# Two elementwise products of chunk 1 moved from VectorE to GpSimd in an attention and two-layer MLP kernel

## The chip, the cores and the metric

The kernel runs on one core of a Trainium2 chip. The metric is the device time of one execution in microseconds (us). The engines are named as in the profile: PE is TensorE (PEld its weight loads), DVE is VectorE, ACT is ScalarE, POOL is GpSimd, and SP is SyncE, which here issues nearly all DMAs. Each engine works through its own queue in order and waits at the head of it for what the instruction needs.

## The reference

A gated linear attention over 768 steps is followed by two MLP layers. Per batch entry and head (4 x 8, width 48), cut to what matters:

```python
mag = np.sqrt(a_re * a_re + a_im * a_im)
scale = np.minimum(mag, 0.999) / (mag + 1e-06)
a_re_n, a_im_n = (a_re * scale, a_im * scale)
for t in range(S):
    new_re = ar * S_re - ai * S_im
    new_im = ar * S_im + ai * S_re
    S_re, S_im = (new_re + kv, new_im)          # kv = outer(k_t, v_t)
    y[:, :, t] = np.einsum('bhd,bhde->bhe', q[:, :, t], S_re)
# the result, as x (3072 x 384), goes through two layers:
h = x @ w_in; x = (h - np.tanh(h)) @ w_out      # layer 0, width 2048
h = x @ w_in; r = np.maximum(h, 0.0); x = (r * r) @ w_out   # layer 1
```

## The kernel before, in words

**Attention.** The 768 steps are cut into 6 chunks of 128. A *unit* is one chunk of one batch entry, so there are 24: unit n has c, b = divmod(n, 4). Chunk 0 is units 0 to 3, chunk 1 is units 4 to 7. In a unit the gate is taken to polar form. Step `a0` loads `ri` (real and imaginary part side by side, 128 x 768). `a1` squares it into `ab`, and `a2` makes on ACT, out of `ab`, one over the real part (tile half `A`). `a3` multiplies the imaginary part by it (`im` times `A`, 128 x 384, in place in `ri`) and bounds the logarithm of the magnitude (`ab<-ab,ri`). `a4` takes the arctangent on ACT (`ri<-ri`), `a5c` adds the phase carried from the chunk before (`ri<-cr,ri`, one partition), `a6l` and `a6` sum along the chunk on PE (`pc` and `pu`), and `a7x` makes the exponentials of the summed logarithm, `ee`. Step `a8x` multiplies the loaded `qk` (q and k, 128 x 768) by `ee` in place. `a9` multiplies by cosine and sine (`kn<-qk,fg`, `qn<-qk,fg`), `a10` transposes on PE (`pk`, `pq`) and ACT copies out (`kqT`), `a11` makes scores (`sc`), which DVE masks (`wm<-sc,maskab`), and `a12` and `a13` make the output `px` and the state's update `pU`.

**MLP.** A block is one of 16 slices m of the hidden width, for one of 6 groups of 512 tokens, in one of 2 layers. Nine products into `h` are followed by tanh on ACT (`t<-h`), a subtraction on DVE (`t<-h,t`), a split into a rounded part `gh` (ACT) and a rest `gl` (DVE), and nine products into `acc`, two blocks later. The `h` tiles of this stage take turns in two PSUM buffers, so the products of block m+2 begin once DVE's `t<-h,t` has read block m's `h`. In layer 0's first group the weights are made meanwhile: per block DVE does one `cv<-st` and two `cv<-st,cv` (128 x 768), ACT a cast to `wh`, and DVE `wl<-cv,wh`.

**What sets the order.** Chunk 1's units are spread over the 16 steps beside layer 0's first group (`plan`, `attn`, `block_step`, tables `AHEAD` and `JOINS`). In this stretch the wrapper `Turn`, which elsewhere forces DVE's and PE's order to be that of the code, is off for all but the last block, so the framework's scheduler orders each engine's queue by its own estimates. Helper `Turn.issue` records all operations on `dve`, `ten`, `sp` and `act_e` under line 155. Tiles tagged `qk` and `ee` have one buffer each outside chunk 0's early units; those tagged `ri` have three. GpSimd clears tiles at the start and splits layer 1's inputs (`xh<-xf`, line 351) six times. In between its queue is empty.

Of the kernel before, what the change touches and what calls it, by code (L numbers as in the profile page):

```python
# [17 lines left out]
ALU = mybir.AluOpType  # L18
# [25 lines left out]
def kernel(  # L44
# [9 lines left out]
    nc = tc.nc  # L54
# [106 lines left out]
    ten, dve, sp = (Turn(e) for e in (nc.tensor, nc.vector, nc.sync))  # L161
# [237 lines left out]
    def unit(n):  # L399
        c, b = divmod(n, B)  # L400
# [10 lines left out]
        V = {}  # L411
# [60 lines left out]

        def a3():
            Bt, im = V["B"], V["im"]
            dve.tensor_tensor(im, im, V["A"], op=ALU.mult)
            dve.scalar_tensor_tensor(
                Bt, Bt, 2.0 * LOG_RMAX, V["X"], op0=ALU.min, op1=ALU.subtract
            )
# [106 lines left out]
                f()  # L585

        def a8x():
            dve.tensor_tensor(V["qk"], V["qk"], V["ee"], op=ALU.mult)


        def a9(pairs=(("kn", "k"), ("qn", "q"))):
# [192 lines left out]
        if c == 0:  # L784
            return dict(
                ld=a0, sq=a1, ln=a2, ph=a3, pc=a6l, ee=a7x, at=a4, pu=a6, rd=a7, lq=l2, lv=l3,
                qe=a8x, sn=a8, er=a7r, kn=lambda: a9((("kn", "k"),)), qn=lambda: a9((("qn", "q"),)),
                t0=t0, e0=t0v, t1=t1_, e1=t1v, s0=lambda: a11((0,)), s1=lambda: a11((1,)),
                m0=lambda: a11v((0,)), m1=lambda: a11v((1,)),
                px=a12, x=a12v, pU=a13, st=a13v, ff=fill,  # L790
            )
        if not packed:
            return [
                (i, dict(p=1, e=5.1, v=5.2, p2=6.1, v2=6.2, k=5.05 if b == B - 1 else 5.1)[kind], f) for i, kind, f in (
                    (0, "e", a0), (1, "e", a1), (2, "e", a2), (3, "e", a3), (4, "e", a3b),
                    (5, "p2", a6l), (6, "e", a7x), (6, "e", l2), (7, "e", a4), (7, "e", a5),
                    (8, "p2", a6), (8, "v2", a7), (10, "e", a8x), (10, "e", a7r),
                    (10 if b == B - 1 else 12, "e", a8), (12, "e", l3), (11 if b == B - 1 else 12, "k", a9),
                    (13, "p", t0), (13, "v", t0v), (13, "p2", t1_), (13, "v2", t1v),
                    (14, "p", a11), (14, "v", a11v), (15, "p", a12), (15, "p", a13),  # L800
                    (15, "v", a12v), (15, "v", a13v),
                )
            ]
# [7 lines left out]
        return [  # L811
            (-1, 2.05, a0), (1, 5.2, a1), ln + (a2,),
            ph + (a3,), (5, 5.1, a3b), (6, 6.3 if late < 2 else 1.1, a6l),
            (6, 1.4, a0c), ex + (a7x,), (7, 6.2, l2), at + (a4,), {0: (9, 5.95), 1: (9, 5.02)}.get(late, (at[0], 7.1)) + (a5c,),
            er + (a7r,), (9, 7.2 if first else 5.3, a5s), (9, 6.9 if late == 1 else 5.4, a8x),
            (10, 6.25 if first else 1.1, a6), (10, 6.26 if first else 1.2, a7),
            (11, 5.15 if first else 1.45, lambda: table("silu_and_others")),
# [9 lines left out]
    for n in range(B, NU):  # L827
        c, b = divmod(n, B)
# [423 lines left out]
```

## Time and profile before

| | us |
|---|---|
| median of 3 runs | 981.78 (981.53 to 982.27) |
| the profiled execution, whole | 981.58 |
| its span, first to last instruction | 979.5 |
| PE busy within it | 950.2 |
| DVE busy | 546.2 |
| ACT busy | 631.6 |
| POOL busy | 19.3 |

About 2 us of an execution lie around the span. PE is busy nearly all the time, DVE and ACT about half of it on average, yet not evenly. A busy time is the union of an engine's instructions, so two that overlap by a little count once. A timeline row gives start, duration, engine and operation, and in brackets how long the engine sat idle before it and what ended that.

### The profile page before, as it was taken

The page shows a single profiled execution, that of the slowest core. Times are in us where ns is not written, and L with a number is a line of the kernel's source. Part 1 is how long each engine was busy: PE and PEld are TensorE (multiplying, and loading weights), DVE is VectorE, ACT ScalarE, POOL GpSimd, SP SyncE. Part 2 cuts the span into 40 slices and gives each one's busy share as a digit, 9 for nine tenths or more (in the row PEclk, how much of TensorE's full clock was granted, in tenths as well). Part 3 has the DMA queues.
Part 4 walks back from the last instruction along what each step waited for, and adds up shares of the span by engine and source line. Part 5 has one row for each costly group of instructions (what it writes and reads, how often), then busy time and mean ns, then how long its engine had stood idle before and what let it go on. Part 6 is the DMA issues. An engine that isn't in the chain of part 4 may idle for free.

```text
span 979.5 us, 18391 instructions
## 1 busy us (share of the span) xinstructions
PE 950.2 (97%) x7424; PEld 785.3 (80%) x7424; DVE 546.2 (56%) x911; ACT 631.6 (64%) x1121; POOL 19.3 (2%) x41
## 2 busy tenths in 40 slices
PE   4999998999999999999999999999999999999997
PEld 1778787878888888888888888888888888888886
DVE  7999997665666666666448995132322322322111
ACT  6789877777777777777534455465666565555442
POOL 2000000000000000000000010000000000000000
PEclk9999999999999999999999999999999999999999
DMA  6544523222322232221127543052444353420000
GB/s 225 171 144 146 175 70 90 75 59 59 90 59 62 71 107 62 62 90 42 57 75 240 188 168 97 1 178 97 151 156 145 97 178 112 129 98 33 33 1 34
DMA packets 56945, 101.01 MB, mean 103 GB/s; under 512 B 23172, under 2 KB 32664, under 8 KB 56856
## 3 DMA queue, kind: packets, MB, share of 16 engines
q1 hardware_dynamic: 56712, 99.67, 32.3%
q8 instruction: 59, 0.97, 0.4%
q14 instruction: 30, 0.25, 0.1%
q10 hardware_dynamic: 144, 0.13, 0.0%
HBM read 87.09 MB, written 9.47 MB: 99 GB/s over the span
## 4 chain that ended last, share of the span: by engine, by line
PE 89%; ACT 5%; DVE 4%; issue 1%; DMA 1%; SPq 0%; ACTq 0%
PE h L155 38%; PE acc L155 38%; PE px L155 4%; PE strips L155 2%; PE pq L155 1%; PE pk L155 1%; ACT L155 1%; PE pU L155 1%; PE sc L155 1%; DVE cv L155 1%; ACT ab L155 1%; PE pu L155 1%; PE pc L155 1%; DMA ri<-in_ri_dram 1%; DVE ab L155 1%
## 5 line engine op out<-in xcount | busy, mean ns | idle before, releaser
L155 DVE TENSOR_TENSOR gl<-t,gh 128x512 fp32r<-128x512 f32 (+1 forms) x193 | 132.3, 685 | 217.2 <-ACT gh L155 216.8
L155 ACT ACTIVATE t<-h 128x512 f32<-128x512 f32 (+1 forms) x193 | 114.6, 594 | 194.3 <-PE h L155 191.7
L155 PE MATMUL h<-xh,wh 128*128 128x512 f32 (+1 forms) x579 | 227.9, 394 | 2.7 <-DVE t L155 2.7
L155 PE MATMUL acc<-gh,wh 128*128 128x512 f32 (+1 forms) x579 | 228.5, 395 | 0.0
L155 PE MATMUL acc<-gh,wl 128*128 128x512 f32 (+1 forms) x579 | 225.7, 390 | 0.0
L155 PE MATMUL acc<-gl,wh 128*128 128x512 f32 (+1 forms) x579 | 225.4, 389 | 0.0
L155 PE MATMUL h<-xh,wl 128*128 128x512 f32 (+1 forms) x579 | 225.3, 389 | 0.0
L155 PE MATMUL h<-xl,wh 128*128 128x512 f32 (+1 forms) x579 | 224.4, 390 | 0.4 <-DVE xl L155 0.4
L155 ACT CAST gh<-t 128x512 fp32r<-128x512 f32 (+1 forms) x191 | 118.0, 618 | 83.7 <-PE acc L155 42.9
L155 PEld LDWEIGHTS h<-xh,wh 128*128 128x128 f32 x579 | 108.8, 188 | 28.7 <-DVE t L155 4.1
L155 PEld LDWEIGHTS h<-xh,wl 128*128 128x128 f32 x579 | 108.8, 188 | 22.8
L155 PEld LDWEIGHTS acc<-gh,wl 128*128 128x128 f32 x579 | 108.8, 188 | 22.5
L155 PEld LDWEIGHTS acc<-gl,wh 128*128 128x128 f32 x579 | 109.0, 188 | 21.7 <-DVE gl L155 0.2
L155 PEld LDWEIGHTS h<-xl,wh 128*128 128x128 f32 x579 | 108.8, 188 | 21.7 <-DVE xl L155 0.6
L155 PEld LDWEIGHTS acc<-gh,wh 128*128 128x128 f32 x579 | 108.9, 188 | 21.2
L155 DVE TENSOR_TENSOR t<-h,t 128x512 f32<-128x512 f32 (+1 forms) x97 | 65.8, 679 | 61.5 <-ACT t L155 61.3
L155 ACT ACT_TABLE_LOAD x64 | 82.1, 1283 | 1.8 <-PEq L1234 0.8
L155 ACT ACTIVATE t<-t 128x512 f32<-128x512 f32 x96 | 60.3, 628 | 1.6
L155 DVE TENSOR_TENSOR wmin<-wmin,cz 128x768 bf16<-128x768 bf16 x32 | 17.8, 557 | 57.5 <-ACT cz L155 57.5
L155 DVE TENSOR_TENSOR wm<-strips,maskab 128x512 f32<-128x512 f32 x32 | 21.8, 690 | 29.8 <-PE strips L155 29.8
L155 DVE SCALAR_TENSOR_TENSOR jw<-st,jw 128x768 int32<-128x768 int32 x32 | 30.4, 950 | 0.2
L155 DVE SCALAR_TENSOR_TENSOR cv<-st,cv 128x768 int32<-128x768 int32 x32 | 30.4, 952 | 0.2
(129 smaller groups left out, 973.4 us busy)
## 6 DMA issues: line engine op xcount, KB each, us to landing
st<-in_w_dram SPq DMA_DIRECT2D x32, 768.0 KB
sr<-in_w_dram SPq DMA_DIRECT2D x32, 768.0 KB
ri<-in_ri_dram SPq DMA_DIRECT2D x24, 384.0 KB
qk<-in_qk_dram SPq DMA_DIRECT2D x24, 384.0 KB
vz<-in_v_dram SPq DMA_DIRECT2D x16, 384.0 KB
x2d<-x2t SPq DMA_DIRECT2D x18, 256.0 KB
xf<-x2d SPq DMA_DIRECT2D x6, 768.0 KB
ss<-in_ri_dram SPq DMA_DIRECT2D x12, 384.0 KB
```

The lines of the kernel that those rows point to most:

```text
L155: r = op(*a, **kw)
```

## The change

In chunk 1's four units, the products of `a3` (`im` times `A`, 128 x 384) and of `a8x` (`qk` times `ee`, 128 x 768) are issued on `nc.gpsimd`. Nothing else of a unit moves to another engine. `nc.gpsimd` isn't wrapped in `Turn`, so these eight instructions carry the lines 476 and 590 instead of 155.

```diff
         def a3():
             Bt, im = V["B"], V["im"]
-            dve.tensor_tensor(im, im, V["A"], op=ALU.mult)
+            e = nc.gpsimd if c == 1 else dve
+            e.tensor_tensor(im, im, V["A"], op=ALU.mult)
...
         def a8x():
-            dve.tensor_tensor(V["qk"], V["qk"], V["ee"], op=ALU.mult)
+            e = nc.gpsimd if c == 1 else dve
+            e.tensor_tensor(V["qk"], V["qk"], V["ee"], op=ALU.mult)
```

GpSimd's queue gets eight rows between its first clears and `xh<-xf`. The number behind a name tells buffers apart: `ri_712` and `qk_854` are unit 4's, `ri_754` and `qk_982` unit 5's, `ri_891` and `qk_1126` unit 6's, `ri_1027` and `qk_1366` unit 7's.

```order
+L476 TENSOR_TENSOR ri_712<-ri_712,ab_716 128x384
+L590 TENSOR_TENSOR qk_854<-qk_854,ee_848 128x768
+L476 TENSOR_TENSOR ri_754<-ri_754,ab_797 128x384
+L476 TENSOR_TENSOR ri_891<-ri_891,ab_928 128x384
+L590 TENSOR_TENSOR qk_982<-qk_982,ee_976 128x768
+L476 TENSOR_TENSOR ri_1027<-ri_1027,ab_1058 128x384
+L590 TENSOR_TENSOR qk_1126<-qk_1126,ee_1120 128x768
+L590 TENSOR_TENSOR qk_1366<-qk_1366,ee_1360 128x768
```

The two kinds of product alternate as the units overlap, and unit 4's `qk` stands ahead of unit 5's `ri`.

The scheduler orders the other queues anew. On DVE, around the `t<-h,t` of block 3 (the last row but one), before `-` and now `+`; `cv_7` and `wl_6` belong to the weights of blocks 7 and 6:

```order
-L155 TENSOR_TENSOR ri_754<-ri_754,ab_797 128x384
 L155 SCALAR_TENSOR_TENSOR ab_797<-ab_797,ri_754 128x384
 L155 SCALAR_TENSOR_TENSOR cv_7_944<-st_7_821,cv_7_944 128x768
 L155 TENSOR_TENSOR wl_6_828<-cv_6_823,wh_6_827 128x768
+L155 SCALAR_TENSOR_TENSOR cv_7_944<-st_7_821,cv_7_944 128x768
 L155 TENSOR_TENSOR t<-h,t 128x512
 L155 SCALAR_TENSOR_TENSOR ri_712<-cr_714,ri_712 1x384
```

A second conversion step of block 7's weights has moved ahead of `t<-h,t`, from the fourth row behind it.

On PE, in the nine products of block 10 into `h` (weights `wh_10`, `wl_10`), where unit 5's transposes `pk` and `pq` lie:

```order
 L155 MATMUL h<-xl_516,wh_10_1232 128x512
 L155 MATMUL h<-xh_515,wl_10_1233 128x512
+L155 MATMUL pk<-ident,kn_1267 96x128 x4
 L155 MATMUL h<-xh_515,wh_10_1232 128x512
+L155 MATMUL h<-xl_516,wh_10_1232 128x512
+L155 MATMUL pq<-ident,qn_1269 96x128 x4
 L155 MATMUL pk<-ident,kn_1267 96x128 x4
-L155 MATMUL h<-xl_516,wh_10_1232 128x512
 L155 MATMUL h<-xh_515,wl_10_1233 128x512
 L155 MATMUL pq<-ident,qn_1269 96x128 x4
```

The first `pk` now stands one product earlier, after the sixth of the nine.

## Rows read from the trace of the kernel before

**Rows 1.** The page's first part: busy us (share of the span) xinstructions.

```profile
PE 950.2 (97%) x7424; PEld 785.3 (80%) x7424; DVE 546.2 (56%) x911; ACT 631.6 (64%) x1121; POOL 19.3 (2%) x41
```

**Rows 2.** Busy us by stretch: PE, PEld, DVE, ACT, POOL, clock, DMA.

```profile
50.00:75.00 25.00, 23.35 (x198) 19.08 (x196) 24.59 (x43) 21.85 (x38) 0.00 (x0) 1.00 0.42 132
...
100.00:125.00 25.00, 23.62 (x218) 18.65 (x216) 24.89 (x39) 21.21 (x35) 0.00 (x0) 1.00 0.58 175
...
300.00:350.00 50.00, 50.00 (x555) 42.20 (x554) 33.46 (x63) 37.28 (x69) 0.00 (x0) 1.00 0.27 73
```

**Rows 3.** Timeline of PE, 60 to 140 us: start, us, instruction, [idle before].

```profile
60.55 0.50 PE L155 MATMUL h<-xh,wh 128*128 128x512 f32 x1 [1.22 <-DVE t L155]
...
71.99 0.40 PE L155 MATMUL h<-xh,wh 128*128 128x512 f32 x1
...
106.48 0.31 PE L155 MATMUL pk<-ident,kn 128*96 128x128 f32 x1 [0.33 <-ACT kqT L155]
...
117.21 0.43 PE L155 MATMUL px<-kqT,state 96*32 96x128 f32 x8 [0.67 <-DVE wm L155]
...
120.14 0.56 PE L155 MATMUL pu<-ri,maskt 128*128 128x384 f32 x1 [0.29 <-PE pU L155]
...
139.45 0.29 PE L155 MATMUL pk<-ident,kn 128*96 128x128 f32 x1 [0.39 <-DVE kn L155]
```

**Rows 4.** Timeline of DVE, 57 to 79 us, some rows.

```profile
57.23 0.56 DVE L155 TENSOR_TENSOR ri<-ri,ab 128x384 f32<-128x384 f32 x1
57.74 0.56 DVE L155 SCALAR_TENSOR_TENSOR ab<-ab,ri 128x384 f32<-128x384 f32 x1
...
68.04 0.55 DVE L155 TENSOR_TENSOR ri<-ri,ab 128x384 f32<-128x384 f32 x1
...
70.25 0.96 DVE L155 TENSOR_TENSOR wl<-cv,wh 128x768 fp32r<-128x768 f32 x1 [0.32 <-ACT wh L155]
71.13 0.68 DVE L155 TENSOR_TENSOR t<-h,t 128x512 f32<-128x512 f32 x1
...
77.75 0.95 DVE L155 TENSOR_TENSOR qk<-qk,ee 128x768 f32<-128x768 f32 x1
78.62 0.55 DVE L155 TENSOR_SCALAR cv<-st 128x768 int32<-128x768 int32 x1
```

**Rows 5.** Timeline of POOL and DVE where both work, 513 and 573 us.

```profile
513.20 0.62 POOL L351 TENSOR_SCALAR xh<-xf 128x512 fp32r<-128x512 f32 x1 [507.28 <-DVE gl L155]
...
513.85 1.09 DVE L155 TENSOR_TENSOR xl<-xf,xh 128x512 fp32r<-128x512 f32 x1 [0.84 <-POOL xh L351]
...
514.36 1.05 POOL L351 TENSOR_SCALAR xh<-xf 128x512 fp32r<-128x512 f32 x1
...
573.94 0.98 DVE L155 TENSOR_SCALAR jw<-st 128x768 int32<-128x768 int32 x1
...
574.85 1.35 DVE L155 TENSOR_TENSOR wl<-jw,wh 128x768 fp32r<-128x768 f32 x1
...
575.36 1.32 POOL L351 TENSOR_SCALAR xh<-xf 128x512 fp32r<-128x512 f32 x1
```

**Rows 6.** Groups of DVE instructions by shape, 50 to 155 us: count, busy us, mean ns.

```profile
L155 DVE TENSOR_TENSOR gl<-t,gh 128x512 fp32r<-128x512 f32 x14 | 9.6, 684 | 0.5 <-ACT gh L155 0.4
L155 DVE TENSOR_SCALAR cv<-st 128x768 int32<-128x768 int32 x12 | 6.6, 557 | 0.0
```

**Rows 7.** Around the moved products: ACT, DVE and PE timelines.

```profile
64.85 0.88 ACT L155 ACTIVATE ee<-pc 128x384 f32<-128x384 f32 x2
...
83.71 0.51 ACT L155 ACTIVATE ri<-ri 128x384 f32<-128x384 f32 x1
...
87.38 0.94 DVE L155 TENSOR_TENSOR kn<-qk,fg 128x768 f32<-128x768 f32 x1
...
104.63 0.39 PE L155 MATMUL pk<-ident,kn 128*96 128x128 f32 x2
```

## The prediction, made before the result was known

> **What bounds the kernel now.** I read the page's first part first: PE is busy 950.2 of 979.5 us [rows 1], so whatever another engine saves can only come out of the 29 us in which PE stands still. The change touches only the time beside layer 0's first group, so the table by stretches comes next. From 300 us on PE is busy all of 50 us out of 50, while in 50 to 75 us and 100 to 125 us it lacks 1.65 and 1.38 us, and there DVE is busy 24.6 and 24.9 of 25 us [rows 2]. Two engines are full at once. DVE has no room, and PE loses a little wherever DVE is late. The timeline of PE then says where: five waits between 60 and 140 us, 1.22, 0.33, 0.67, 0.29 and 0.39, together 2.9 us [rows 3]. Those of 1.22, 0.67 and 0.39 us ended with an instruction of DVE inside the stretch that the change lightens (`t`, `wm`, `kn`). The waits of 0.33 and 0.29 us are for ACT's copies and PE's own results. So the most that relief on DVE can bring is about 2.3 us, 0.2% of the time, which is about what a measurement of this kernel can tell from no change. A loss has no such limit.
>
> **What is removed.** On DVE a product of 384 columns lasts 0.55 us and the next instruction starts 0.51 us after it (57.23 to 57.74), one of 768 columns 0.95 and 0.87 us (77.75 to 78.62) [rows 4]. Four of each are 4 x (0.51 + 0.87) = 5.5 us of DVE's queue.
>
> **What is added.** No row shows a product of two tensors on GpSimd. The nearest is `xh<-xf`, one input, 512 columns, 0.62 us when DVE leaves it alone [rows 5]. The users are far off. Unit 5's `im` product ran at 68.04 us [rows 4] and its arctangent at 83.71, unit 4's `qk` product at 77.75 and its first use, `kn`, at 87.38 [rows 4, 7]. So the product's own length, be it 1 or 2 us, is covered by 9 us of other work, and so is its standing in line: unit 4's `qk` stands ahead of unit 5's `im` in GpSimd's queue, and even 2 us of it end long before 83 us. Behind a late `kn` on DVE would stand `qn` and the weights of block 9, and PE's transposes would wait for it; with that cover they don't. Neither step issues a DMA, and SP's queue is asked for nothing new beyond waiting for GpSimd before it reloads `qk`.
>
> **What it costs DVE.** While GpSimd runs `xh<-xf`, DVE's instructions stretch: `xl<-xf,xh` 1.09 us where an equal shape takes 0.684, `jw<-st` 0.98 where it takes 0.557, `wl<-jw,wh` 1.35 where the like `wl<-cv,wh` takes 0.96 [rows 4 to 6]. Each time that is 0.39 to 0.42 us for one GpSimd instruction of 512 columns, and GpSimd's own rows stretch from 0.62 to 1.05 and 1.32 us. Both can't read SBUF through the same port at once, and one waits for the other. The Trainium skill says so in "SBUF — State Buffer", section "Who interferes with whom": a DVE instruction with two SBUF inputs and a GpSimd instruction that reads SBUF exclude each other, and the second to start waits for the whole of the first; the rows agree.
>
> So each moved product takes time from DVE again. At the pace of one input, 0.42 us for 512 columns, that is 0.32 us for 384 and 0.63 for 768, a lower bound. At the longest row, 1.32 us for 512, it is 0.99 and 1.98, an upper one. A product reads two tensors, so I take twice the one-input pace, 0.64 and 1.26 us, an estimate. Four units then cost DVE 4 x 1.90 = 7.6 us where 5.5 were saved (bounds 3.8 and 11.9). The nearest row bounds this below the saving, so a gain isn't excluded. The Trainium skill's "GPSIMD Engine Reference", section "Elementwise — side-by-side cycle accounting", speaks against the change: it has a two-input GpSimd instruction at 4497 ns for 2048 columns, about twice DVE's; by that, an estimate, the two are 0.84 and 1.69 us, and place A below alone would come to +2.9 us and the sum to about +3.3; no row of this trace shows a two-input GpSimd instruction.
>
> **Where it reaches PE.** Place A is the first product of block 5 at 71.99 us, which needs `t<-h,t` of block 3, done at 71.13 + 0.68 = 71.81 [rows 3, 4]. That margin is 0.18 us. Ahead of that `t`, two 384-column products go (-0.51, -0.47 from 68.04 us on), DVE's wait of 0.32 us for ACT vanishes, and a conversion of block 7's weights is moved ahead of it (+0.87). That alone would be -0.43 us. Three GpSimd products, `im` of units 4 and 5 and `qk` of unit 4, the first and last ready where DVE made them at 57.23 and 68.04, the `qk` one when `ee` is done at 65.73 [rows 4, 7], add 0.64 + 1.26 + 0.64 = 2.54. PE is later by 2.1 us (one-input pace: +0.8; upper bound: +3.5).
>
> Place B is `px` of unit 4. Unit 5's `qk` product on DVE, 0.87 us between two masks, goes, and GpSimd's 1.26 us falls at the same place, since `qk` is reloaded only after unit 4's `qn`. At 0.39 more, with PE's part now asked for earlier, I take +0.5 (0 to 1.3). Place C is unit 5's first `pk`, at 104.63 us [rows 7]. It now stands one product earlier, and more weight conversion stands ahead of `kn`. DVE has been set back by six GpSimd products by then, against which 3.7 us were removed. I take +1.0 (0 to 2). In place D the change helps: the waits of 0.67 us for `wm` and 0.39 us for `kn` go, since unit 6's `qk` no longer stands ahead of `wm` and a later PE finds `kn` ready, -1.1. From 300 us on PE is full [rows 2], so what is lost by then isn't given back.
>
> Sum: 2.1 + 0.5 + 1.0 - 1.1 = +2.5 us. On the profiled execution's own 981.58 us that gives 984.1; the median of the runs is 0.2 us above it, which I leave in the range.
>
> **The rivals.** (1) *Relief, faster.* If a two-input product on GpSimd doesn't hold DVE's reads, place A gives -0.4, place D -1.1, and B and C nothing: 980.1 us. It decides if DVE's `wl` and `cv` beside a GpSimd product keep 0.95 us. The rows of 513 and 573 us speak against it; that the gained waits are real speaks for it. (2) *It cancels, no change.* At the one-input pace place A is +0.8, B and C are 0 to 0.5, D is -1.1: about 981.8. The same comes out if many GpSimd products fall beside DVE instructions that read PSUM (`t<-h,t`, `wm`), which don't meet them. For it: DVE does weights early, so not each delay reaches PE. (3) *Heavier.* At the longest row's pace: A +3.5, B +1.3, C +2.0, D -1.1, 987.3 us. For it: at 575.36 us GpSimd was held as well. (4) The moved products become late themselves, GpSimd's order making `kn` wait. With 9 us of cover I give it nothing of its own.
>
> **How the numbers follow.** Forecast (A to D at twice the pace, 982.5 to 985.7) 0.45, relief 0.15, cancelling 0.30, heavier 0.10. 0.2% is 1.96 us, so 983.74 us is the edge of slower. Of the forecast 0.10 falls under it. Slower: 0.35 + 0.10 = 0.45; within: 0.30 + 0.10 = 0.40; faster: 0.15. Signs are mixed, so the forecast's own range stands above; the range reaches from relief's value, 980.2, to within the heavier case, 986.8.
>
> **What would show it.** In the profile of the changed kernel: eight GpSimd products, those of 768 columns 1.3 us or longer; DVE's `cv`, `wl` or `gl` stretched beside each of them; the wait of PE at block 5's first product, near 72 us, from nothing to about 2 us for DVE's `t`; no wait of `px` for `wm` near 117 us. PE's busy time stays. If DVE's rows stay at 0.95 us and PE's waits between 55 and 155 us shrink, the forecast falls. If the products are long but PE waits no longer in sum, the cost was hidden by DVE's early weights.

## The result and the profile after

The changed kernel took 990.7 us (986.95 to 992.58, 6 runs) beside 982.0 us for the kernel before in the same comparison: a ratio of 1.0088, interval 1.0073 to 1.0103. It is slower, as held likeliest, but by 8.7 us where 2.5 were forecast, and the time lies above the range. The profiled execution took 991.87 us, 10.3 more than that of before. The page's first part answers [rows 1]:

```profile
PE 954.4 (96%) x7424; PEld 786.7 (79%) x7424; DVE 549.6 (56%) x903; ACT 630.8 (64%) x1121; POOL 33.7 (3%) x49
```

DVE has eight instructions fewer and yet 3.4 us more busy time. The table by stretches answers [rows 2]; its columns are busy us of PE, PEld, DVE, ACT and POOL, then granted clock and DMA:

```profile
50.00:75.00 25.00, 21.58 (x182) 17.25 (x175) 24.99 (x38) 21.05 (x36) 4.93 (x3) 1.00 0.37 127
75.00:100.00 25.00, 23.89 (x216) 19.16 (x214) 24.50 (x37) 22.38 (x37) 3.54 (x3) 1.00 0.54 175
100.00:125.00 25.00, 21.56 (x195) 16.55 (x192) 21.00 (x32) 18.76 (x32) 4.12 (x2) 0.86 0.46 138
```

PE lacks 3.42 and 3.44 us in the first and third stretch, where it lacked 1.65 and 1.38. In the third the granted clock is also down, to a mean of 0.86. The timeline of POOL shows the eight products:

```profile
56.91 1.63 POOL L476 TENSOR_TENSOR ri<-ri,ab 128x384 f32<-128x384 f32 x1 [50.98 <-ACT ab L155]
65.54 2.01 POOL L590 TENSOR_TENSOR qk<-qk,ee 128x768 f32<-128x768 f32 x1 [7.00 <-ACT ee L155]
67.51 1.33 POOL L476 TENSOR_TENSOR ri<-ri,ab 128x384 f32<-128x384 f32 x1
82.46 1.15 POOL L476 TENSOR_TENSOR ri<-ri,ab 128x384 f32<-128x384 f32 x1 [13.62 <-ACT ab L155]
95.29 2.21 POOL L590 TENSOR_TENSOR qk<-qk,ee 128x768 f32<-128x768 f32 x1 [11.69 <-DMA qk<-in_qk_dram]
99.82 1.32 POOL L476 TENSOR_TENSOR ri<-ri,ab 128x384 f32<-128x384 f32 x1 [2.31 <-ACT ab L155]
112.93 2.97 POOL L590 TENSOR_TENSOR qk<-qk,ee 128x768 f32<-128x768 f32 x1 [11.79 <-DMA qk<-in_qk_dram]
133.96 2.01 POOL L590 TENSOR_TENSOR qk<-qk,ee 128x768 f32<-128x768 f32 x1 [18.06 <-DMA qk<-in_qk_dram]
```

Beside each of them one instruction of DVE is stretched. DVE's timeline, the rows at those times, and `t` of block 3:

```profile
57.59 1.36 DVE L155 SCALAR_TENSOR_TENSOR ab<-ab,ri 128x384 f32<-128x384 f32 x1
65.76 2.21 DVE L155 TENSOR_SCALAR cv<-st 128x768 int32<-128x768 int32 x1
67.89 1.76 DVE L155 SCALAR_TENSOR_TENSOR cv<-st,cv 128x768 int32<-128x768 int32 x1
73.25 0.68 DVE L155 TENSOR_TENSOR t<-h,t 128x512 f32<-128x512 f32 x1
82.76 1.66 DVE L155 SCALAR_TENSOR_TENSOR cv<-st,cv 128x768 int32<-128x768 int32 x1
96.33 1.60 DVE L155 SCALAR_TENSOR_TENSOR ab<-ab 128x384 f32<-128x384 f32 x1
100.28 1.28 DVE L155 SCALAR_TENSOR_TENSOR ab<-ab,ri 128x384 f32<-128x384 f32 x1
114.76 1.56 DVE L155 SCALAR_TENSOR_TENSOR ab<-ab 128x384 f32<-128x384 f32 x1
134.19 2.19 DVE L155 SCALAR_TENSOR_TENSOR ab<-ab 128x384 f32<-128x384 f32 x1
```

Against 0.55 to 0.56 us (`ab`), 0.56 (`cv<-st`) and 0.95 (`cv<-st,cv`) undisturbed, the four beside 384-column products lose 0.80, 0.81, 0.71 and 0.73 us, the four beside 768-column products 1.65, 1.05, 1.01 and 1.64: 8.4 us together, where 7.6 were forecast and 5.5 saved. The timeline of PE answers [rows 3], its rows from 57 to 150 us with a wait of half a us or more, and at 60.21 block 2's first product, whose wait for block 0's `t` was 1.22 us before:

```profile
59.10 0.88 PE L155 MATMUL pc<-ab,maskab 128*128 128x384 f32 x2 [0.91 <-DVE ab L155]
60.21 0.50 PE L155 MATMUL h<-xh,wh 128*128 128x512 f32 x1 [0.23 <-DVE t L155]
...
73.98 0.50 PE L155 MATMUL h<-xh,wh 128*128 128x512 f32 x1 [1.54 <-DVE t L155]
87.75 0.91 PE L155 MATMUL pu<-ri,maskt 128*128 128x384 f32 x2 [0.59 <-DVE ri L155]
98.59 0.74 PE L155 MATMUL px<-wm,vz 128*32 128x128 f32 x18 [0.53 <-DVE wm L155]
108.84 0.61 PE L155 MATMUL pk<-ident,kn 128*96 128x128 f32 x4 [1.05 <-DVE kn L155]
...
116.95 1.93 PE L155 MATMUL px<-kqT,state 96*32 96x128 f32 x32 [2.34 <-ACT ee L155]
...
147.75 0.61 PE L155 MATMUL pk<-ident,kn 128*96 128x128 f32 x4 [1.50 <-DVE kn L155]
```

The longest wait, 2.34 us, isn't for DVE at all. The timeline of ACT says what `ee` itself waited for:

```profile
112.68 0.85 ACT L155 ACTIVATE ab<-ri 128x768 f32<-128x768 f32 x1
115.94 0.87 ACT L155 ACTIVATE ee<-pc 128x384 f32<-128x384 f32 x2 [2.41 <-POOL qk L590]
```

This `ee` is unit 7's. The tile has one buffer, so it can't be written before the product of unit 6 has read unit 6's `ee`. That product starts at 112.93, once its `qk` is reloaded, and lasts 2.97 us. ACT stands still for 2.41 us, the PSUM tile `pc` that this `ee` reads isn't free, and PE's `px`, one of the tiles that take turns with `pc` in three PSUM places, waits behind it.

The new order of the queues has a part in this. Before, unit 6's product ran on DVE, and unit 7's `ee` came after it, no earlier than now (DVE's and ACT's timelines of before):

```profile
115.52 0.95 DVE L155 TENSOR_TENSOR qk<-qk,ee 128x768 f32<-128x768 f32 x1
116.67 0.85 ACT L155 ACTIVATE ee<-pc 128x384 f32<-128x384 f32 x2
```

But 26 products into `acc` and `h` stood between the scores `sc` and this `px`, at 117.21 [rows 3], and kept PE busy. In the new order only one stands there, so PE asks for the place before `ee` has been made.

Then the clock falls. The changed kernel was run and profiled again (`after_b`, below), and there the same wait of 2.33 us was not followed by a lower clock. The tables by stretches, first the profile above, then the second one:

```profile
108.00:112.00 4.00, 3.11 (x21) 2.60 (x22) 4.00 (x6) 3.29 (x6) 0.00 (x0) 1.00 0.40 130
112.00:116.00 4.00, 2.61 (x19) 2.02 (x17) 4.00 (x6) 1.59 (x4) 2.97 (x1) 1.00 0.55 219
116.00:120.00 4.00, 3.05 (x35) 2.50 (x36) 2.77 (x6) 3.98 (x9) 0.00 (x0) 0.57 0.55 169
120.00:124.00 4.00, 4.00 (x33) 2.77 (x35) 2.27 (x5) 1.72 (x2) 0.00 (x0) 0.58 0.21 35
```

```profile
108.00:112.00 4.00, 3.31 (x22) 2.60 (x22) 4.00 (x7) 3.28 (x7) 0.00 (x0) 1.00 0.42 146
112.00:116.00 4.00, 2.43 (x19) 2.01 (x17) 4.00 (x6) 1.59 (x4) 3.08 (x1) 1.00 0.47 181
116.00:120.00 4.00, 3.24 (x42) 2.64 (x42) 2.77 (x6) 3.98 (x9) 0.00 (x0) 1.00 0.58 194
120.00:124.00 4.00, 4.00 (x91) 3.23 (x89) 3.97 (x9) 3.96 (x7) 0.00 (x0) 1.00 0.18 14
```

In the first the clock is near the lower level, 1.2 GHz, for most of 116 to 124 us, after 8 us in which PE was busy 5.7; in the second it stays at 2.4 GHz after 8 us with 5.7 as well. What it costs is read from the same two groups of `px` in both timelines. First those of the first profile (its earlier one, at 116.95, stands above), then of the second:

```profile
123.38 1.08 PE L155 MATMUL px<-wm,vz 128*32 128x128 f32 x32
```

```profile
116.76 1.08 PE L155 MATMUL px<-kqT,state 96*32 96x128 f32 x32 [2.33 <-ACT ee L155]
...
120.29 1.08 PE L155 MATMUL px<-wm,vz 128*32 128x128 f32 x32
```

From one to the other it is 6.43 us against 3.53: 2.9 us lost to the clock.

### The profile page after: what moved, and what is told of

It is laid out like the page before. It is cut to its first block, busy times and chain, and to the rows that moved or that the text cites. A ratio compares the mean times of both kernels' runs of the same rounds, so it can differ in the third digit from the quotient of the medians.

```text
span 989.8 us, 18406 instructions
## 1 busy us (share of the span) xinstructions
PE 954.4 (96%) x7424; PEld 786.7 (79%) x7424; DVE 549.6 (56%) x903; ACT 630.8 (64%) x1121; POOL 33.7 (3%) x49
## 4 chain that ended last, share of the span: by engine, by line
PE 82%; DVE 13%; ACT 2%; issue 1%; DMA 1%; POOL 0%; SPq 0%; DVEq 0%; POOLq 0%; ACTq 0%
PE acc L155 35%; PE h L155 34%; PE px L155 4%; DVE jw L155 3%; DVE cv L155 2%; PE strips L155 2%; DVE wl L155 2%; PE pk L155 1%; PE pq L155 1%; DVE gl L155 1%; DVE t L155 1%; PE pU L155 1%; PE sc L155 1%; PE pu L155 1%; DVE ab L155 1%
## 5 line engine op out<-in xcount | busy, mean ns | idle before, releaser
L351 POOL TENSOR_SCALAR xh<-xf 128x512 fp32r<-128x512 f32 x18 | 14.0, 805 | 696.7 <-DVE gl L155 385.9
```

What stands on the lines that cost most here:

```text
L351: nc.gpsimd.tensor_scalar(xh[:, kk], xf[:, kk], 1.0, 0.0, op0=ALU.mult, op1=ALU.add)
```

## The experiments

Two theories for the 6.6 us beyond the forecast, and later a third. **E**: the event of the single `ee` buffer, the wait and the half clock behind it. **P**: GpSimd's holds on DVE alone, heavier or more often on PE's path than reckoned. **L**: the products' own length and late results. "Before" is that of the same comparison, 981 to 982 us.

**Is it the `ee` buffer?** `ee2` gives `ee` two buffers. Room for it was made by keeping the carried phase `cr` in a row that the units share, so a unit may add another unit's phase.

```diff
...
-            pair("ee", "E1", "E2")
+            pair("ee", "E1", "E2", bufs=2)
...
-            V["cr"] = ap1.tile([1, HD], F32, tag="cr", name=f"cr{n}")
+            V["cr"] = crow[:1]
```

> The changed kernel with two buffers for the tile of exponentials (ee) in place of one; to make room, the one-row tile cr is put into the tile crow as a further row. The queues of PE and DVE keep the order that they have in the changed kernel. Theory E (buffer): most of the loss is one event near unit 6, where ACT stands 2.4 us because unit 7's ee may not be written until GpSimd has read unit 6's, PE stands behind it and its clock falls. Then this run loses that event and only the waits at block 5 and at unit 5's transposes stay: about 984.5 us, no half-clock stretch between 100 and 130 us. Theory P (port): the loss comes from DVE being held 8.4 us in sum by GpSimd's reads, spread over all four units. Then the time stays at 988 to 991 us.

`u6_dve` removes the reader instead; the scheduler then orders DVE and PE a little differently too:

```diff
-            e = nc.gpsimd if c == 1 else dve
+            e = nc.gpsimd if c == 1 and b != 2 else dve
             e.tensor_tensor(V["qk"], V["qk"], V["ee"], op=ALU.mult)
```

> The changed kernel with unit 6's qk product alone put back on DVE; seven products stay on GpSimd. Theory E (buffer): about 984.5 us, as GpSimd no longer reads unit 6's ee late. Theory P (port): one of eight holds goes (1.0 of 8.4 us) and 0.87 us comes back to DVE, so 989 to 990.5 us.

Measured: `ee2` 986.9 us, ratio 1.0050 (1.0033 to 1.0066); `u6_dve` 986.6 us, 1.0044 (1.0030 to 1.0059). Both lie between the theories: the wait for `ee` is gone and about 4 us with it, but 4 to 5 stay. So `ee` isn't most of the loss, as E had it. `u6_dve`'s table by stretches shows the clock drop once more, at another place, after PE had waited 1.59 us for `wm` at 99 us:

```profile
75.00:100.00 25.00, 22.83 (x128) 18.26 (x132) 24.51 (x38) 22.02 (x37) 2.96 (x2) 0.98 0.54 174
100.00:125.00 25.00, 24.95 (x307) 20.95 (x300) 24.72 (x39) 22.60 (x39) 1.64 (x1) 0.95 0.45 139
```

**A cleaner form.** `ee6w` lays only unit 6's `ee` into a place that is free then. Apart from `ee` of unit 6 standing one row earlier on ACT, all queues are those of the changed kernel.

```diff
-                t = pool.tile([P, n2], F32, tag=name, name=f"{name}_{n}", bufs=bufs)
+                w = n == 6 and name == "ee"; t = (wpool if w else pool).tile([P, n2], F32, tag=f"wl{NM - 1}" if w else name, name=f"{name}_{n}", bufs=bufs)
```

> The changed kernel, but unit 6's ee lies in a tile of its own (the place of block 15's wl, free then), so that ACT may write unit 7's ee at once. The queues of PE, DVE, GpSimd and SP are row for row those of the changed kernel; on ACT one row (unit 6's ee) stands one place earlier. Nothing is left out. Theory E (the single ee buffer): the wait of 2.3 us of px for ACT's ee and the half-clock stretch behind it go, 986.0 to 987.5 us, as with two ee buffers. Theory P (only the holds on DVE count, and the ee wait merely stood ahead of DVE waits that would have come anyway): 989 to 991 us.

> The same kernel as ee6w again, for more runs beside those of hold and of the changed kernel: 985.5 to 987.0 us. Theory E (wait for ee and the half clock behind it make the difference to the changed kernel): mean granted clock 0.998 to 1.00 in most runs. Theory P: as the changed kernel, 989 to 991 us.

> The changed kernel again, for more runs: 990 to 991 us. Theory E: the runs fall into two groups, near 987.5 us where the mean granted clock is 0.998 or more and near 992 us where it is 0.993 to 0.995, so that the half-clock stretch is worth about 4 us and the wait for ee itself 1 to 2. Theory N (the clock has nothing to do with it): time and mean clock are unrelated.

Measured: `ee6w` 986.0 us, 1.0055 (1.0033 to 1.0076), and again 986.4 us, 1.0056 (1.0043 to 1.0069). The changed kernel beside the latter: 987.8 us (987.64 to 993.2), 1.0085 (1.0065 to 1.0104). By the ratios the single buffer costs 0.0029 of the time, 2.8 us; the two intervals touch and the medians are 1.4 us apart, so the size is known to a few us only. E holds, but for about a third of the loss. `ee6w`'s list of PE's waits, 50 to 160 us, has none for ACT's `ee` before `px` any more:

```profile
PE px L155 <- DVE wm L155: 0.9, 2, 0.5
```

Part of the difference is the clock. Of 12 runs of the changed kernel, five had a mean granted clock of 0.998 or more and took 987.8 us on average, seven had less and took 990.9. Of 10 runs of `ee6w` six had 0.998 or more, with 985.7 us, and four had less, with 987.7. The kernel before, split in the same way in each comparison, differs by 0.4 to 1.0. Where the clock was high the two kernels differ by 2.0 us, about the wait of 2.3. The two clean groups that were expected for the changed kernel did not come: two runs at 0.997 took 987.8 and 989.5 us, and the median lay below the 990 to 991 expected. Nor does the lower clock belong to `ee` alone: in `ee6w_b`'s profile, without that wait, it was 0.97 and 0.96 in 75 to 100 and 100 to 125 us, after PE had waited 1.62 us for `wm`.

**Which products?**

`im_only` and `qk_only` move one kind alone, `qk4_only` and `qk6_only` one product alone.

```diff
+            e = nc.gpsimd if c == 1 and b == 2 else dve
             e.tensor_tensor(V["qk"], V["qk"], V["ee"], op=ALU.mult)
```

That is `qk6_only`, with `im` left on DVE; `qk4_only` has `b == 0`, `qk_only` `c == 1` alone, and in `im_only` it is the other way round. The scheduler orders DVE and PE anew in each of them, so that each time holds a product's cost together with that of an order of its own.

> Only the product of the imaginary part (128x384) goes to GpSimd; q, k times the exponentials stays on DVE. Theory E (buffer): no GpSimd instruction reads ee, so no long wait of ACT; about 982 to 983.5 us. Theory P (port): four holds of about 0.76 us, 3.0 us against 2.0 us saved, a little over a third of the loss: about 985 us.

> Only the product of q, k with the exponentials (128x768) goes to GpSimd. Theory E (buffer): the wait of ACT for GpSimd at unit 6 stays, and with it most of the loss: 987 to 990 us, with a half-clock stretch after it. Theory P (port): four holds of 1.0 to 1.65 us, 5.3 us against 3.5 us saved, about two thirds of the loss: 987 us, without the wait being needed for it.

> Of the eight products only unit 4's of 768 columns is on GpSimd, the rest on DVE as before. Theory A (my place A: two parts of GpSimd's hold ahead of block 3's subtraction cost PE time that nothing gives back): PE waits 1 to 1.5 us more for t near 72 us, 983.0 to 983.7 us. Theory C (DVE's early weights absorb one product's hold of 1.65 us against the 0.87 us removed): 981.8 to 982.6 us.

> Of the eight products only unit 6's of 768 columns is on GpSimd, the rest on DVE as before. Theory E (the ee event is worth 4 us by itself, wait and half clock): px waits 2 to 4 us for ACT's ee near 115 us, a half-clock stretch follows, 985.5 to 987.0 us. Theory P (it needs DVE to be late already from the other seven): 982.0 to 983.5 us, no half clock.

| | us | ratio (interval) |
|---|---|---|
| `im_only` | 983.0 | 1.0013 (1.0002 to 1.0024) |
| `qk_only` | 990.8 | 1.0082 (1.0063 to 1.0101) |
| `qk4_only` | 982.9 | 1.0010 (0.9999 to 1.0021) |
| `qk6_only` | 984.9 | 1.0036 (1.0025 to 1.0048) |

The 768-column products bring nearly all; `im_only` is where E had it, below the 985 of P. Unit 4's alone costs about 1 us, at the edge of what can be told, and its 982.9 lies between the two theories' ranges. Its timeline of PE speaks for theory A, with a wait for `t` where before had none:

```profile
73.35 0.50 PE L155 MATMUL h<-xh,wh 128*128 128x512 f32 x1 [0.97 <-DVE t L155]
```

Unit 6's alone costs 3.5, between the two theories' ranges, and the `ee` event is there without any DVE delay by the other seven. ACT and PE of `qk6_only`:

```profile
110.49 0.87 ACT L155 ACTIVATE ee<-pc 128x384 f32<-128x384 f32 x2 [2.44 <-POOL qk L590]
```

```profile
111.50 1.08 PE L155 MATMUL px<-kqT,state 96*32 96x128 f32 x32 [1.63 <-ACT ee L155]
```

No half clock followed in its profile, so E's wait came out, and E's clock did not. In `qk_only` the wait is 3.5 us, and its third stretch has the lower clock:

```profile
100.00:125.00 25.00, 19.93 (x179) 14.88 (x181) 21.07 (x32) 18.36 (x31) 4.84 (x1) 0.86 0.44 138
```

**What is the other part?** `none` leaves the eight products out altogether: chunk 1's q and k don't get the exponentials, and its imaginary parts aren't divided. Its queues on PE, DVE, ACT and SP are, row for row, those of `ee6w`. It shows what relief and the new order bring together.

```diff
+            if c != 1:
                 dve.tensor_tensor(im, im, V["A"], op=ALU.mult)
...
+            if c != 1:
                 dve.tensor_tensor(V["qk"], V["qk"], V["ee"], op=ALU.mult)
```

> The kernel before with the eight products of chunk 1 left out altogether (the exponentials then don't reach q and k of chunk 1, and its imaginary parts aren't divided), so DVE is relieved of 5.5 us and GpSimd does nothing. Theory R (what the relief can bring at most, from the waits for DVE of the trace before): 979.5 to 980.5 us. Theory S (the scheduler's new order and PE's own work leave nothing of it): 981.5 to 982.5 us.

> The kernel without the eight products again, as the base of hold1q and hold2q on the same chip: 980.5 to 981.5 us.

`hold` adds to `none` GpSimd work that nothing is meant to wait for, on a scratch tile, at the products' places, `im`'s and then `qk`'s in the diff. `hold1q` is `hold` with no reader of `ee` left after unit 4, `hold2q` has twice the work.

```diff
...
+            if c == 1:
+                nc.gpsimd.tensor_tensor(scr[:, :1], im[:, :1], V["A"][:, :1], op=ALU.mult)
+                nc.gpsimd.tensor_tensor(scr, scr, scr, op=ALU.mult)
...
+            if c == 1:
+                nc.gpsimd.tensor_tensor(scr[:, :1], V["qk"][:, :1], V["ee"][:, :1], op=ALU.mult)
+                for _ in range(2):
+                    nc.gpsimd.tensor_tensor(scr, scr, scr, op=ALU.mult)
```

> The kernel without the eight products (as in none: the exponentials don't reach q and k of chunk 1, and its imaginary parts aren't divided), but GpSimd squares a scratch tile of its own where each product stood: 128x384 once in place of an im product, twice in place of a qk product, each set off by a one-column product that reads the product's inputs. The queues of PE, DVE, ACT and SP are row for row those of none and of ee6w, so it holds DVE as the changed kernel does, yet nothing waits for GpSimd. Theory P (beyond the ee event, the loss is time in which GpSimd holds DVE's instructions): as ee6w, 985.0 to 987.0 us, PE's waits for DVE 5 to 7 us between 50 and 160 us. Theory L (it is the products' own length and their late results): as none, 980.5 to 982.0 us.

> As hold (the eight products left out, GpSimd squares its own tile in their places), but the one-column product that sets off unit 5's, 6's and 7's scratch work reads qk alone, so that not even ACT's ee can wait for it. Queues of PE, DVE, ACT and SP as before. Theory P: DVE's rows between 50 and 160 us are stretched by 2 to 3 us in sum, and the time is 2 us above the kernel without products, 982.5 to 983.5 us. Theory L: as the kernel without products, 980.5 to 981.5 us.

> As hold1q with the scratch work doubled: two squares of 128x384 in place of an im product, four in place of a qk product, queues of PE, DVE, ACT and SP the same. Theory P (what GpSimd takes of DVE's time is lost about one for one): DVE's rows stretched by 5 to 6 us in sum, 984.5 to 986.5 us, near the changed kernel with unit 6's ee apart. Theory L: as the kernel without products, 980.5 to 981.5 us.

All but before have the same queues on PE and DVE. "DVE stretched" sums, over DVE's groups of one shape between 50 and 160 us, count times (mean less the shortest mean in before or `none`). "PE idle" is 100 us less PE's busy time, from 50 to 150 us of the profile.

| | us | ratio (interval) | DVE stretched | PE idle |
|---|---|---|---|---|
| `none` | 981.1 | 0.9997 (0.9986 to 1.0008) | 0.6 | 3.6 |
| `none_b` | 980.1 | 0.9984 (0.9975 to 0.9993) | 0.2 | 2.7 |
| `hold` | 983.2 | 1.0021 (1.0012 to 1.0030) | 3.1 | 5.7 |
| `hold1q` | 983.9 | 1.0022 (1.0013 to 1.0031) | 3.8 | 5.2 |
| `hold2q` | 986.8 | 1.0047 (1.0033 to 1.0061) | 8.8 | 8.2 |
| `ee6w_b` | 986.4 | 1.0056 (1.0043 to 1.0069) | 9.4 | 8.4 |
| changed (`after_b`) | 987.8 | 1.0085 (1.0065 to 1.0104) | 7.5 | 9.2 |
| before | 981.6 | 1 | 0.1 | 3.5 |

DVE's groups of one shape (count, busy us, mean ns), of `none_b`, `hold1q` and `hold2q`, the two that stretch most in `hold1q`; in `hold2q` `gl<-t,gh` and `ab<-ab,ri` add 2.7 us:

```profile
L155 DVE SCALAR_TENSOR_TENSOR cv<-st,cv 128x768 int32<-128x768 int32 x24 | 22.7, 951 | 0.1
L155 DVE TENSOR_TENSOR wl<-cv,wh 128x768 fp32r<-128x768 f32 x13 | 12.4, 952 | 1.4 <-ACT wh L155 1.4
```

```profile
L155 DVE SCALAR_TENSOR_TENSOR cv<-st,cv 128x768 int32<-128x768 int32 x25 | 25.6, 1027 | 0.1
L155 DVE TENSOR_TENSOR wl<-cv,wh 128x768 fp32r<-128x768 f32 x13 | 13.7, 1053 | 1.3 <-ACT wh L155 1.1
```

```profile
L155 DVE SCALAR_TENSOR_TENSOR cv<-st,cv 128x768 int32<-128x768 int32 x25 | 25.6, 1028 | 0.1
L155 DVE TENSOR_TENSOR wl<-cv,wh 128x768 fp32r<-128x768 f32 x13 | 15.2, 1167 | 0.5 <-ACT wh L155 0.5
```

Twice the GpSimd work, which no engine needs, costs 1.7 times as much: from `none_b` +3.7 us for 3.6 us of stretched rows, and +6.2 for 8.6 (ratios times 982). Both stretched more than expected (2 to 3 and 5 to 6 us). `ee6w_b` with 9.2 us is +7.1, in line with that, and in its profile, from 50 to 160 us, no idle time of PE, DVE or ACT is ended by GpSimd. In PE's timelines between 55 and 145 us the waits for DVE come to 1.9 us in `none_b` and 6.6 in `ee6w`. So theory P holds for the larger part and L falls. One blot: in `hold` itself a one-column product was held 1.52 us and `px` waited 0.7 us for GpSimd; `hold1q`, without that, gave the same time. The holds of `hold` were a third of the real products' for the same columns, which is why it landed between the theories.

No version of this move that was run beats the kernel before: even with the products gone, the gain is 0.3 (`none`, within the noise) to 1.6 us (`none_b`). The first lies between the theories R and S, the second with R.

## Why the prediction was wrong

**What the 8.7 us are.** The relief gives 0.3 to 1.6 us (`none`). The holds on DVE take 5.7 to 7.1 us from there to `ee6w`, with the lower clock of some of its runs in it. The single `ee` buffer takes about 2.8 more.

**The failed step** is place D, a gain of 1.1 us that became a loss of 2.8, and under it the step on the product's length: "covered by 9 us of other work", with rival 4, to which I gave nothing. I looked for those who read the product's result, `kn` and the arctangent, and there the cover was real: no wait for a product's result shows in `ee6w`. I did not look for who must write what the product reads. `ee` has one buffer, as the section on the kernel says, and the next unit's exponential stands in ACT's queue right behind. The two numbers were in reach: a product that can't start before the `qk` reload, and an `ee` of the next unit that comes due meanwhile. Nor did I follow `px` in PE's new queue, where it had moved ahead of 25 products. No run has GpSimd's product in the old order, so the order's share in the wait isn't measured. Without the `ee` event the time, 986.0 and 986.4 us, lies in the range, near its upper end.

**The clock** wasn't in the sum. PE at 1.2 GHz for most of 8 us cost 2.9 us in the profiled run, and eight us at 0.57 lower the mean of the whole run by 0.0035. In the five of 12 runs at 0.998 or more it can't have been that long. So the profiled execution, 991.87 us, shows the loss near its largest.

**Place A** came out: block 5's first product started at 73.98 where it was 71.99 [rows 3], 2.0 us later (2.1 forecast), with `t` at 73.25 instead of 71.13 [rows 4]. The wait shown is 1.54, since PE itself came later.

**Places B and C**: `px` waited 0.53 us for `wm` (0.5 forecast), unit 5's `pk` 1.05 for `kn` (1.0). Up to 109 us the forecast stood.

**Place D** had the wrong sign, by more than its size. The wait of 0.67 us for `wm` [rows 3] became one of 2.34 for `ee`, and that of 0.39 for `kn` [rows 3] became 1.50 at 147.75. With 2.8 us instead of -1.1 it is the term with the largest error, 3.9 us. In `ee6w`, without the `ee` event, the two are 0.36 for `wm` and 1.50 for `kn`, still +0.8. `none` shows that the second half was wrong even without GpSimd: there PE waits 1.3 us for `kn`, 0.4 before unit 5's transposes and 0.9 before unit 7's, where before had 0.39 (the list of PE's waits, 50 to 160 us):

```profile
PE pk L155 <- DVE kn L155: 1.3, 2, 0.9
```

With A 2.0, B 0.5, C 1.05, `pu`'s new wait of 0.59 at 87.75, D 2.8 and the clock 2.9 the sum is 9.8 of the 10.3 us between the two profiled executions.

**The size of the hold** was near: 8.4 us in the stretched rows where I took 7.6. A product of 384 columns held DVE by 0.76 us on average (0.64 taken), one of 768 by 1.34 (1.26). The Trainium skill's "GPSIMD Engine Reference", section "Elementwise — side-by-side cycle accounting", gave 0.84 and 1.69 when scaled by columns, an estimate of GpSimd's own time. The trace has more: even the shortest products took 1.15 and 2.01 us, what DVE held of them included. Taken as a hold, as the prediction did, 1.69 is near the longest rows, 1.64 and 1.65, and above the mean. At 65.76 us DVE's `cv` starts 0.2 us behind GpSimd's product, which ends at 67.55, and ends 0.4 us after that. The other seven rows end 0.4 us behind their product too, those of `cv<-st,cv` 0.8. The rest of the first was waited for each time; the Trainium skill's "SBUF — State Buffer", section "Who interferes with whom", calls the shared pair of ports an exclusive lock, and the rows agree.

**The rivals.** Relief: the gain of 1.5 us is what `none_b` gives (1.6), and its condition, no hold, isn't met. Cancelling fell: all eight products met an instruction that they stretched, though unit 6's also lay beside a `t<-h,t` (114.16 us) that kept its 0.68. Heavier, 987.3 us, is near what `ee6w` gave (986.0 and 986.4), but by more places, not by longer holds.

**What stays open.** Why 5.5 us less in DVE's queue are worth 0.3 to 1.6 us, while a us of hold costs 0.7 to 1. The scheduler's new order is the same in `none` and seems to eat part of the relief: PE's waits for DVE between 55 and 145 us are 1.9 us in `none_b` beside 2.3 before [rows 3], for those of `t` and `wm` shrink and new ones for `t` (0.29) and `kn` (0.39, and 0.88 instead of 0.39) appear. But no run had the old order without products. And why the clock fell in one profile of the changed kernel and not in the other, with the same waits.

## What to carry to other kernels

When an instruction moves to a slower engine, list who reads its result and also who next writes each of its inputs; a single-buffered input can make that writer, on a third engine, wait, and its queue carries the wait to PE. Look in the new order of the queues, too, for who now asks earlier for what that writer makes. Work on GpSimd beside a full DVE isn't relief: here DVE got more stretch (8.4 us) than it was spared work (5.5). Test such a claim with a dose, work that nobody needs in unchanged queues, since that separates the hold from the order and from late results.

## What the runs showed of the hardware

A one-column product on GpSimd took from 0.19 to 2.13 us in `hold`. The long one ended at 59.64 us, 0.05 after the last of four instructions of DVE on two SBUF tiles each, which ran from 56.44 to 59.59; so GpSimd is held as DVE is (timeline of POOL of `hold`):

```profile
57.51 2.13 POOL L478 TENSOR_TENSOR scr<-ri,ab 128x1 f32<-128x1 f32 x1 [51.23 <-ACT ab L155]
...
94.21 0.19 POOL L595 TENSOR_TENSOR scr<-qk,ee 128x1 f32<-128x1 f32 x1 [10.57 <-DMA qk<-in_qk_dram]
```

A wait of PE of 2.3 us can be followed by a stretch at the lower clock that costs a further 2.9 us, and need not be. After one of 1.6 us for `wm` the clock fell in `u6_dve` and `ee6w_b`, and did not in `ee2`. Squaring one scratch tile in place stretched DVE by 2.5 to 3.6 us for the columns for which the products, of two tiles, stretched it by 7 to 9; no run tells whether the operands or the places make that difference.
